# Three chained layers on one core: engine orders planned from a recorded list of operations

## The chip, the cores and the metric

The kernel runs on one core of a Trainium2 chip, in float32 from end to end. The metric is device time in microseconds of that core; three runs before the change gave 747.24 us as their median (746.17 to 747.3).

## The reference

Three layers follow each other, for batch 4, 768 positions and 384 channels: a gated linear recurrence with 8 heads of 48 channels, attention with four experts of which each position uses two, and a two-layer MLP with a residual.

```python
for t in range(S):                                   # recurrence, 8 heads
    state = alpha[:, :, t, :, None] * state + k[t] outer v[t]
    y[:, :, t] = q[t] @ state
logits = x @ w_gate                                  # x: y, heads side by side
w = softmax over the two largest logits
for e in range(4):                                   # causal attention, one head of 64 each
    a = softmax(causal((x @ wq[e]) @ (x @ wk[e]).T / 8))
    out += w_e * (a @ (x @ wv[e]) @ wo[e])
xn = layer_norm(out) * g_ln
return out + relu(xn @ w_ch1) @ w_ch2                # 384 -> 1536 -> 384
```

## The kernel before, in words

**Recurrence.** It is computed in 24 chunks of 128 positions (4 batches by 6). For a chunk, `gla_a` makes the running product of the gates (a scan on VectorE, L199), its inverse by a logarithm and an exponential on ScalarE (L201, L202), and scales keys and queries (L203 to L206, partly on GpSimd). `gla_b` multiplies keys by queries (L221) with 48 rows of the array in use, two heads side by side in its upper and lower half, masks the product (L225) and transposes the keys (L230). `gla_c` updates the state (L244, L254, L255) and computes the chunk's output (L263) with 32 columns of the array in use, four products side by side. `qkv` projects two chunks at a time to queries, keys and values (L304, L318).

**Attention.** The 48 units are pairs of experts in one block of 128 query positions (`UN`). `scores` (L432) has 64 rows of the array in use, two experts side by side; the maximum is taken on VectorE (L438, L440) and the exponential on ScalarE (L442). `transp` transposes the result (L464) and `av` multiplies it with the values (L487), 64 columns in use, again two experts side by side; L490 spreads the weights. `wout` (L505) projects the result and stores it to a buffer in DRAM.

**MLP.** 12 blocks of 256 positions: layer norm and its transposes (L611), first product (L631), second product (L648). Its weights arrive as 64-bit floats and are split into two 32-bit parts by `conv` on VectorE, ScalarE and GpSimd (L536 to L550); the first weight goes through DRAM.

**Products.** Where both operands carry 32 bits in full, as in L221, L244, L263, L487 and L490, a matmul of the program shows as two records in the trace. Projections and MLP instead split each operand in a high and a low part and use three matmuls for a product.

**What sets the order.** The program issues its operations in an order in which recurrence and MLP are generators that are pulled a little at a time between the steps of the attention units (`fill`, `pull`, `need`). That is not yet the order of the engines: the context is made with `schedule_with_timeline_sim=True` (L818), and the library's scheduler sorts every engine's instructions by its own model of times. Only the matmuls of `av` are held together by `manual_schedule` (L482). In this text a **mode** of TensorE is one of four ways in which the array is used: full (128 rows, 128 columns), half (up to 64 rows: L221, L432), pair (64 columns: L487, L490) and quad (32 columns: L263). A **switch** is a place in TensorE's order where a matmul of one mode follows one of another.

```python
            for n, (qt, kt) in enumerate(((QH, KH), (QL, KH), (QH, KL))):
                for h in range(2):
                    pe.matmul(P[h][x], qt[rs[h], p, qs], kt[rs[h], p, pw * x:pw * x + pw], ...)   # L432
...
        with tc.manual_schedule(engines={mybir.EngineType.PE}):                                   # L482
...
    with tile.TileContext(nc, schedule_with_timeline_sim=True) as tc:                             # L818
```

Of the kernel before, what the change touches and what calls it, by code (L numbers as in the profile page):

```python
# [21 lines left out]
PF0 = 0.05  # L22
PF1 = 0.98
NA = 4
NAT = 2
MB = 1.0
MB0 = -10000
TM = 4
KP = 0
NF = 8  # L30
LA = 2
SB = 0
KP2 = 1
GE = 1
PS1 = 1
RRE = 0
OLE = 0
CVU = 33
GQ = 0
GST = 0  # L40
HS = 2
EO = 0
LO = 1
OL = 1
CV0 = 0
GAT = 0
G0 = 1
SW = 1
NWU = 40
AF0 = 0  # L50
RB = 2
CB = 1
NB = 1
W2 = 384
CR = 5
B, H, S, D = 4, 8, 768, 48
DM = H * D
# [6 lines left out]
CW = AW + 2 * 512  # L64

# [4 lines left out]

@with_exitstack
def kernel(ctx: ExitStack, tc: tile.TileContext, akq, vd, wqkv, wo, g_ln, w1, w2, out):
    nc = tc.nc
    pe, dve, act, pool, sp = nc.tensor, nc.vector, nc.scalar, nc.gpsimd, nc.sync

# [4 lines left out]
    psF = ctx.enter_context(tc.tile_pool(name="psF", bufs=NF, space=PSUM))  # L80
    att_ps = ExitStack()
    gen_st = [ExitStack()]
    gen_pool = {}
    gen_pool[1] = ctx.enter_context(tc.tile_pool(name="gen1", bufs=1))
    gen_pool[0] = gen_st[0].enter_context(tc.tile_pool(name="gen0", bufs=1, side="right"))
    fill_st = ExitStack()
# [3 lines left out]
    xs = dram.tile([B, S, DM], F32, name="xs")  # L90
# [3 lines left out]
    psx = {}  # L94

    def psf():
        return psF.tile([128, 512], F32, tag="F", name="F")

    def psm():
        return psx["p"].tile([128, 512], F32, tag="X", name="X") if psx and NF < 5 else psf()  # L100

    ld = [gl.tile([128, CW], F32, name=f"ld{i}") for i in range(4)]
    vb = [gl.tile([128, 4, 2, 2, 32], F32, name=f"vb{i}") for i in range(3)]
    st = [gl.tile([128, 4, 3, 32], F32, name=f"st{i}") for i in range(2)]

    def load_sc(c):
        b, s = divmod(c, NSC)
        sp.dma_start(ld[c % 4], akq[b, s])

    def load_vb(c):  # L110
        b, s = divmod(c, NSC)
        sp.dma_start(vb[c % 3].rearrange("p j x h e -> p (j x h e)"), vd[b, s])

    def new_gen(b):
        p = gen_pool[b % 2]
        if (b % 2, "t") not in GEN:
            GEN[b % 2, "t"] = (*(p.tile([128, 2, S], FR, name=f"{n}{b % 2}") for n in ("QH", "QL", "KH", "KL")),
                               p.tile([128, NSC, E * HD + E], F32, name=f"V{b % 2}"),
                               p.tile([128, NSC, E], F32, name=f"W{b % 2}"))
        GEN[b] = GEN[b % 2, "t"]  # L120
# [5 lines left out]
    GEN = {}  # L126
    wraw = []
    for k in range(KT):
        t = aw.tile([128, 772], F32, name="A", bufs=NA)
        sp.dma_start(t, wqkv[:, k])  # L130
        wraw.append(t)
# [3 lines left out]
    gsb = const.tile([128, KT], F32, name="gsb")  # L135
    sp.dma_start(gsb, g_ln)

    ident = const.tile([128, 128], F32, name="ident")
    make_identity(nc, ident)
    for _ in range(NWU // 4):  # L140
        P = psf()
        for x in range(4):
            pe.transpose(P[:, 128 * x:128 * x + 128], ident, ident)
    hot = gl.tile([128, 4, 129], F32, name="hot")
    pool.memset(hot, 0.0)
    pool.memset(hot[:, :, 0:1], 1.0)
    for t in st:
        pool.memset(t, 0.0)
    gmask = gl.tile([128, 128], F32, name="gmask")
    pool.memset(gmask, -1.0)  # L150
    pool.affine_select(out=gmask, in_=gmask, pattern=[[1, 128]], compare_op=OP.is_ge, fill=0.0, base=0,
                       channel_multiplier=-1)
    cmask = const.tile([128, 512], BF, name="cmask")
    pool.memset(cmask, 0.0)
    pool.affine_select(out=cmask[:, 384:], in_=cmask[:, 384:], pattern=[[-1, 128]], compare_op=OP.is_ge, fill=-1e9, base=0,
                       channel_multiplier=1)
    tri = const.tile([128, 4, 4], F32, name="tri")
    pool.memset(tri, 1.0)
    pool.affine_select(out=tri, in_=tri, pattern=[[1, 4], [-1, 4]], compare_op=OP.is_gt, fill=0.0, base=0,
                       channel_multiplier=0)  # L160

    g20 = const.tile([128, KT], F32, name="g20")
    pool.tensor_scalar(g20, gsb, 2.0 ** -20, 0.0, op0=OP.mult, op1=OP.add)

    WH = gl.tile([128, KT, 772], FR, name="WH")
    WL = gl.tile([128, KT, 772], FR, name="WL")
    OWH = const.tile([128, 2, DM], FR, name="OWH")
    OWL = const.tile([128, 2, DM], FR, name="OWL")

    def split_w():  # L170
        for k in range(KT):
            act.activation(WH[:, k], wraw[k], AF.Copy)
            (dve if SW else pool).tensor_tensor(WL[:, k], wraw[k], f(WH[:, k]), op=OP.subtract)
        if not OL:
            load_wo()

    def load_wo():
        oraw = aw.tile([128, 2 * S], F32, name="at", bufs=NAT)[:, :2 * DM].rearrange("p (k c) -> p k c", k=2)
        sp.dma_start(oraw, wo)
        act.activation(OWH, oraw, AF.Copy)  # L180
        pool.tensor_tensor(OWL, oraw, f(OWH), op=OP.subtract)

    G = {}
    SM = {}
    XT = {}

    def gla_a(c):
        s = c % NSC
        t = ld[c % 4]
        al = t[:, 0:AW]  # L190
        q = t[:, AW:AW + 512].rearrange("p (j t) -> p j t", j=4)
        k = t[:, AW + 512:].rearrange("p (j t) -> p j t", j=4)
        gt = gw.tile([128, 4, 129], F32, name="gt", bufs=3)
        gi = gw.tile([128, 4, 129], F32, name="gi")
        gm = al[:, :512].rearrange("p (j t) -> p j t", j=4)
        G[c] = gt
        for j0, j1 in (((0, 2), (2, 4)) if c < HS else ((0, 4),)):
            js = slice(j0, j1)
            dve.tensor_tensor_scan(gt[:, js].rearrange("p j t -> p (j t)"), al[:, 129 * j0:129 * j1],  # L199
                                   hot[:, js].rearrange("p j t -> p (j t)"), 0.0, op0=OP.mult, op1=OP.add)  # L200
            act.activation(gi[:, js], gt[:, js], AF.Ln)  # L201
            act.activation(gi[:, js], gi[:, js], AF.Exp, scale=-1.0)  # L202
            (dve if c < G0 else pool).tensor_tensor(gm[:, js], gt[:, js, 1:], gi[:, js, 1:], op=OP.mult)  # L203
            (pool if KP else dve).tensor_tensor(k[:, js], k[:, js], gi[:, js, 1:], op=OP.mult)
            dve.scalar_tensor_tensor(k[:, js], gm[:, js], 2.0, k[:, js], op0=OP.subtract, op1=OP.mult)
            (dve if GQ else pool).tensor_tensor(q[:, js], q[:, js], gt[:, js, 1:], op=OP.mult)  # L206

    def qk_of(c):
        t = ld[c % 4]
        q = t[:, AW:AW + 512].rearrange("p (j t) -> p j t", j=4)  # L210
        k = t[:, AW + 512:].rearrange("p (j t) -> p j t", j=4)
        return q, k

    def gla_b(c):
        q, k = qk_of(c)
        SM[c] = gw.tile([128, 2, 4, 128], F32, name="smk")
        P = [psf().rearrange("p (j t) -> p j t", j=4) for h in range(2)]
        for j in range(4):
            for h in range(2):
                r = slice(64 * h, 64 * h + 48)  # L220
                pe.matmul(P[h][:, j], k[r, j], q[r, j], start=True, stop=True)  # L221
            if j == 1:
                yield 850
        for h in range(2):
            dve.tensor_tensor(SM[c][:, h], P[h], gmask[:, None, :].to_broadcast([128, 4, 128]), op=OP.mult)  # L225
        yield 850
        if c % NSC < NSC - 1:
            P = psf()
            for j in range(4):
                pe.transpose(P[:, 128 * j:128 * j + 128], k[:, j, :], ident)  # L230
            kt = gw.tile([128, 4, 128], F32, name="kt")
            act.activation(kt.rearrange("p j t -> p (j t)"), P, AF.Copy, scale=-1.0)
            G[c, "kt"] = kt
            yield 430

    def gla_c(c):
        s = c % NSC
        q, k = qk_of(c)
        v = vb[c % 3]
        if s < NSC - 1:  # L240
            P = psf()
            kt = G.pop((c, "kt"))
            for j in range(4):
                pe.matmul(P[:, 128 * j:128 * j + 128], kt[:, j, :], v[:, j].rearrange("p x h e -> p (x h e)"), start=True, stop=True)  # L244
            P = P.rearrange("p (j b e) -> p j b e", j=4, b=4)
            new = st[(c + 1) % 2]
            for h in range(2):
                r = slice(64 * h, 64 * h + 48)
                bs = slice(h, 3, 2 - h)
                gl_b = G[c][r, :, 128:129, None].to_broadcast([48, 4, 2, 32])  # L250
# [14 lines left out]
        for T in range(2):  # L265
            jobs = []
            for n in range(4):
                j, h = 2 * T + n // 2, n % 2
                l = [(v[:, j, 0, h], sm[:, h, j])]
                if s:  # L270
                    l.append((sto[:112, j, h], q[:112, j]))
# [4 lines left out]
        for j in range(4):  # L276
            l = [(v[:, j, 1, h], sm[:, h, j]) for h in range(2)]
            if s:
                l.append((sto[:112, j, 2], q[:112, j]))
# [481 lines left out]
    for _ in bk:  # L761
        pass
# [59 lines left out]
```

## Time and profile before

| what | value |
|---|---|
| median of three runs | 747.24 us |
| span of the profiled execution (the page gives no other time of it) | 749.8 us |
| TensorE (PE) busy | 713.5 us, 95% |
| VectorE (DVE) busy | 447.5 us, 60% |
| ScalarE (ACT) busy | 308.5 us, 41% |
| GpSimd (POOL) busy | 174.5 us, 23% |
| matmul records | 6520 |
| mean granted TensorE clock | 0.970 of full |

Matmuls are pipelined: one record reaches from a matmul's start to its modelled end, and the next starts long before that. So the busy share of TensorE says that it is rarely without work and not how fast it works; for that one reads the distance from one start to the next.

### The profile page before, as it was taken

What the parts mean: (1) busy time and instruction counts of PE and PEld (TensorE: products, weight loads), DVE (VectorE), ACT (ScalarE), POOL (GpSimd) and SP (SyncE); (2) the same over time, 40 slices, a digit from 0 to 9 for tenths busy, and PEclk for the clock granted to TensorE, in tenths of its full rate; (3) what the DMA queues carried; (4) which work ended last, traced back from release to release, by engine and by line L of the source; (5) the groups of instructions that cost most, each with busy time, mean ns of one, the idle gap of its engine ahead of it and who ended that gap; (6) DMA issues with size and microseconds to landing.
All of it is one profiled execution on the core that took longest, in us unless ns stands there. A gap on an engine that the chain in (4) does not pass through costs nothing.

```text
span 749.8 us, 16242 instructions
## 1 busy us (share of the span) xinstructions
PE 713.5 (95%) x6520; PEld 643.2 (86%) x6520; DVE 447.5 (60%) x1241; ACT 308.5 (41%) x879; POOL 174.5 (23%) x284
## 2 busy tenths in 40 slices
PE   7599799989989999999899999999999999999998
PEld 6488678868868788779678888999999999999997
DVE  6757787767897787766678954254245335433521
ACT  3324455545555555555567545232223123212310
POOL 4624345243464334321223221000000000000000
PEclk8688999999999999999999999999999999999999
DMA  8113424233322622211932311001100100110100
GB/s 338 71 57 115 151 68 138 98 117 121 121 97 96 208 61 83 77 41 54 323 99 79 96 43 55 22 32 43 43 11 33 43 22 22 43 43 12 32 22 22
DMA packets 30427, 60.87 MB, mean 81 GB/s; under 512 B 2960, under 2 KB 19856, under 8 KB 30352
## 3 DMA queue, kind: packets, MB, share of 16 engines
q1 hardware_dynamic: 18864, 45.68, 18.3%
q10 hardware_dynamic: 8352, 9.44, 3.6%
q0 software_dynamic: 3136, 4.72, 2.3%
q8 instruction: 51, 0.84, 0.5%
q14 instruction: 24, 0.20, 0.1%
HBM read 45.67 MB, written 14.16 MB: 80 GB/s over the span
## 4 chain that ended last, share of the span: by engine, by line
PE 69%; DVE 9%; DMA 7%; ACT 4%; POOL 3%; issue 3%; SPq 0%; ACTq 0%; POOLq 0%; DVEq 0%
PE F L631 21%; PE F L648 20%; PE F L304 5%; PE F L487 5%; PE F L432 4%; PE F L464 3%; DMA ld<-in_akq_dram 3%; PE F L505 2%; DMA raw<-in_w_dram 2%; DVE gt L199 2%; PE F L263 2%; PE F L318 2%; PE F L221 1%; ACT A L442 1%; PE F L244 1%
## 5 line engine op out<-in xcount | busy, mean ns | idle before, releaser
L635 ACT ACTIVATE hh<-F 128x256 fp32r<-128x256 f32 x144 | 55.0, 384 | 196.6 <-PE F L631 196.0
L631 PE MATMUL F<-nh,w1hl 128*128 128x256 f32 x864 | 129.0, 284 | 0.0
L631 PEld LDWEIGHTS F<-nh,w1hl 128*128 128x128 f32 x864 | 114.4, 191 | 1.7 <-issue 0.7
L648 PE MATMUL F<-w2h,hh 128*128 128x384 f32 x288 | 98.8, 343 | 0.0
L648 PE MATMUL F<-w2l,hh 128*128 128x384 f32 x288 | 97.0, 337 | 0.0
L648 PE MATMUL F<-w2h,hl 128*128 128x384 f32 x288 | 96.9, 336 | 0.0
L636 DVE SCALAR_TENSOR_TENSOR hl<-F,hh 128x256 fp32r<-128x256 f32 x144 | 60.1, 419 | 56.8 <-ACT hh L635 56.3
L442 ACT ACTIVATE A<-F,nm 128x384 f32<-128x384 f32 (+4 forms) x128 | 68.4, 541 | 52.7 <-DVE nm L440 44.4
L652 DVE TENSOR_TENSOR xt<-F,xt 128x384 f32<-128x384 f32 x24 | 13.4, 558 | 110.5 <-PE F L648 110.5
L631 PE MATMUL F<-nl,w1hl 128*128 128x256 f32 x432 | 75.5, 283 | 0.0
L487 PE MATMUL F<-at,V 128*64 128x128 f32 x672 | 62.1, 286 | 2.3 <-ACT at L467 1.6
L631 PEld LDWEIGHTS F<-nl,w1hl 128*128 128x128 f32 x432 | 62.2, 192 | 0.2 <-issue 0.2
L487 PEld LDWEIGHTS F<-at,V 128*64 128x64 f32 x672 | 41.5, 137 | 19.1 <-issue 7.5
L464 PE MATMUL F<-ident,A 128*128 128x128 f32 x336 | 54.5, 284 | 3.3 <-DVE rb L494 2.6
L648 PEld LDWEIGHTS F<-w2h,hh 128*128 128x128 f32 x288 | 54.2, 188 | 1.1 <-issue 0.8
L648 PEld LDWEIGHTS F<-w2l,hh 128*128 128x128 f32 x288 | 54.2, 188 | 0.2
L648 PEld LDWEIGHTS F<-w2h,hl 128*128 128x128 f32 x288 | 54.1, 188 | 0.2 <-issue 0.2
L464 PEld LDWEIGHTS F<-ident,A 128*128 128x128 f32 x336 | 37.9, 142 | 12.6 <-issue 5.0
L221 PE MATMUL F<-ld 48*128 48x128 f32 x384 | 37.8, 309 | 9.1 <-issue 5.1
L221 PEld LDWEIGHTS F<-ld 48*128 48x128 f32 x384 | 30.2, 203 | 15.4 <-issue 9.8
L206 POOL TENSOR_TENSOR ld<-ld,gt 128x512 f32<-128x512 f32 (+1 forms) x26 | 30.2, 1166 | 56.4 <-DVE gt L199 29.1
L467 ACT ACTIVATE at<-F 128x512 f32<-128x512 f32 (+1 forms) x72 | 38.7, 542 | 6.6 <-PE F L464 4.8
(185 smaller groups left out, 1420.9 us busy)
## 6 DMA issues: line engine op xcount, KB each, us to landing
ld<-in_akq_dram SPq DMA_DIRECT2D x24, 770.0 KB, 4.8
vb<-in_vd_dram SPq DMA_DIRECT2D x24, 256.0 KB, 2.8
raw<-in_w_dram SPq DMA_DIRECT2D x18, 256.0 KB, 2.7
wsc<-whl ACTq DMA_DIRECT2D x18, 256.0 KB, 2.4
xs<-xo ACTq DMA_DIRECT2D x24, 192.0 KB, 1.9
w1hl<-wsc POOLq DMA_DIRECT2D x4, 1152.0 KB, 14.9
xt<-xs SPq DMA_DIRECT2D x24, 192.0 KB, 2.5
raw<-in_w_dram SPq DMA_DIRECT2D x12, 384.0 KB, 3.2
```

The lines of the kernel that those rows point to most:

```text
L206: (dve if GQ else pool).tensor_tensor(q[:, js], q[:, js], gt[:, js, 1:], op=OP.mult)
L221: pe.matmul(P[h][:, j], k[r, j], q[r, j], start=True, stop=True)
L304: pe.matmul(P[:, mt % 2], wt[:, k, cs], x[:, k], start=(n == 0), stop=(n == 8))
L432: pe.matmul(P[h][x], qt[rs[h], p, qs], kt[rs[h], p, pw * x:pw * x + pw], start=(n == 0), stop=(n == 2), skip_group_check=True)
L442: act.activation(A[h][:, pw * x:pw * x + pw], t, AF.Exp, bias=nm[:, h:h + 1], scale=1.0 if x < npc - 1 else -1.0, accum_out=dn2[:, h, x:x ...
L464: pe.transpose(P[:, 128 * n:128 * n + 128], A[h][:, 128 * x:128 * x + 128], ident)
L467: act.activation(at[:, cs], P[:, :128 * len(g)], AF.Copy)
L487: pe.matmul(O[64 * h:64 * h + 64, :], V[:, x, HD * e:HD * e + HD], at[:, c:c + 128], start=(x == 0), stop=(x == i), skip_group_check=True)
L631: pe.matmul(P, w[:, k, c], x[:, k], start=(n == 0), stop=(n == 8))
L635: act.activation(hh, P, AF.Relu)
L636: dve.scalar_tensor_tensor(hl, P, 0.0, f(hh), op0=OP.max, op1=OP.subtract)
L648: pe.matmul(P, x[:, o], w[:, ff], start=(ff == 0 and n == 0), stop=(ff == KF - 1 and n == 2))
```

## The change

The kernel is written again around a recorder. Every operation (or a group of matmuls that belong together) becomes an `Op` with an engine, a duration, a function that issues it, and the tiles or parts of tiles that it reads and writes. `Plan.run` then goes through time: for each engine it takes, from the operations whose inputs are ready and whose buffers are free, the one that stands first in the order in which the program recorded them, adds its duration from the table, and issues it. For TensorE it prefers an operation of the present mode as long as one of another mode isn't more than 4,000 ns of TensorE work ahead of it in the recorded order (`STICK`), and waits up to 60 ns for one (`LOOK`); a switch costs in the table 95 ns and 27 to 107 ns by mode. The result is taken as it stands: the whole kernel is under `manual_schedule()`.

```diff
+STICK = 4000.0
+LOOK = 60.0
+LOAD = {"full": 90.0, "half": 107.0, "quad": 27.0, "pair": 53.0}
+CHANGE = 95.0
...
+            if e == "PE":
+                s, o = min(((s, o) for s, o in cand if s <= t0 + (LOOK if o.mode == mode else 0.0)),
+                           key=lambda x: (x[1].pos + (STICK if x[1].mode != mode else 0.0), x[1].n))
+            else:
+                s, o = min(((s, o) for s, o in cand if s <= t0), key=lambda x: (x[1].pos, x[1].n))
...
+            if e == "PE" and o.mode != mode:
+                ns += CHANGE + LOAD[o.mode]
+                mode = o.mode
...
-        raw = p.tile([128, cw, 2], I32, name="raw", bufs=RB)
-        if i == 0:
-            pool.tensor_copy(raw[0:1, 0, 0:1].bitcast(F32), M["nm"][0:1, 0:1])
...
-    with tile.TileContext(nc, schedule_with_timeline_sim=True) as tc:
-        tile_gla_moe_attention_mlp_kernel(tc, *args)
+    with tile.TileContext(nc, schedule_with_timeline_sim=True) as tc:
+        with tc.manual_schedule():
+            tile_gla_moe_attention_mlp_kernel(tc, *args)
```

TensorE, VectorE, ScalarE and SyncE have the same number of instructions as before, with the same DMAs. GpSimd has 19 fewer: the 18 copies that held back the loads of the first MLP weight (L526) and one unused scaling (L163). On TensorE the switches are 155 where they were 358: ahead of the first output projection 23 (45 before), from there to the last projection to values 92 (217), after that 40 (96).

The first place is TensorE at the last projections of the recurrence (L304 and L318, now L491 and L512), between them attention's transposes (L464, now L644) and its products with the values (L487, now L669). Before:

```order
L304 MATMUL F<-xl,WH 128x256 x3
L487 MATMUL F<-at,V_377 64x128
L318 MATMUL F<-WH,xh 128x260 x3
L318 MATMUL F<-WL,xh 128x260 x3
L318 MATMUL F<-WH,xl 128x260
L487 MATMUL F<-at,V_377 64x128 x7
L490 MATMUL F<-ident,rr 64x128 x2
L318 MATMUL F<-WH,xl 128x260 x2
L464 MATMUL F<-ident,A 128x128 x4
```

And now:

```order
L491 MATMUL F<-xh,WH 128x256 x3
L491 MATMUL F<-xh,WL 128x256 x3
L491 MATMUL F<-xl,WH 128x256 x3
L669 MATMUL F<-at,V_108 64x128 x6
L672 MATMUL F<-ident,rr 64x128 x2
L601 MATMUL F<-KH_106,QH_104 128x512 x2
```

One unit's products with the values stood in two pieces, of one and of seven matmuls, among the projections (four switches), and now stand in one piece, behind the projections and ahead of the next scores. Over the whole program the products with the values (L487, L490) and with the keys of the recurrence (L221) stood in pieces of an odd number of matmuls, in which one has no partner beside it, 68 times before; now they do nowhere.

The second place is TensorE in the stretch behind the recurrence, where only attention is left until the MLP starts: scores (L432, now L601), transposes, products with the values and output projections (L505, now L691). Before:

```order
L432 MATMUL F<-KL_376,QH_373 128x384
L464 MATMUL F<-ident,A 128x128 x6
L487 MATMUL F<-at,V_377 64x128
L464 MATMUL F<-ident,A 128x128 x4
L487 MATMUL F<-at,V_377 64x128 x6
L432 MATMUL F<-KH_1409,QH_1407 128x384
```

And now:

```order
L691 MATMUL F<-OWL,oh 128x384 x2
L691 MATMUL F<-OWH,ol 128x384 x2
L644 MATMUL F<-ident,A 128x128 x18
L669 MATMUL F<-at,V_108 64x128 x8
L672 MATMUL F<-ident,rr 64x128 x2
L601 MATMUL F<-KH_106,QH_104 128x384 x2
```

Transposes of two units now stand together, 18 in a row (20 at the longest), where they stood in pieces of four and six.

The third place is VectorE near the start, where the scan (L341, was L199) and the state updates (L421, was L254) of the first chunks stand. Now:

```order
L461 TENSOR_TENSOR xl<-F,xh 128x3x128
L717 TENSOR_SCALAR cva<-raw 128x256
L719 SCALAR_TENSOR_TENSOR cva<-raw,cva 128x256
L352 SCALAR_TENSOR_TENSOR ld_89<-ld_89,gi 128x512
L421 TENSOR_TENSOR st_94<-st_93,F 48x4x2x32
L341 SCALAR_TENSOR_TENSOR gt<-ld_86,hot 128x516
```

The conversion of the first piece of MLP weight (L717, was L536) has moved in among the fourth chunk's work; before, it stood behind the first unit's scores.

## Rows read from the trace of the kernel before

**Rows 1.** The page: span, and busy time, share and instructions of each engine.
```profile
span 749.8 us, 16242 instructions
PE 713.5 (95%) x6520; PEld 643.2 (86%) x6520; DVE 447.5 (60%) x1241; ACT 308.5 (41%) x879; POOL 174.5 (23%) x284
```
**Rows 2.** Busy time by stage; PEclk is the granted clock (1.00 is full).
```profile
core 0: us, PE busy (x) PEld busy (x) DVE busy (x) ACT busy (x) POOL busy (x), PEclk, DMA share, GB/s
20.00:100.00 80.00, 65.58 (x721) 56.05 (x714) 55.48 (x128) 30.02 (x77) 33.51 (x45) 0.82 0.28 97
100.00:200.00 100.00, 95.48 (x1116) 80.00 (x1116) 76.55 (x199) 51.16 (x146) 44.31 (x66) 0.98 0.33 108
200.00:300.00 100.00, 94.83 (x1127) 80.02 (x1125) 79.93 (x210) 54.11 (x152) 42.78 (x65) 0.98 0.34 114
300.00:400.00 100.00, 96.30 (x941) 77.18 (x940) 68.50 (x236) 58.12 (x181) 26.13 (x60) 0.98 0.39 116
400.00:480.00 80.00, 80.00 (x631) 70.80 (x632) 51.78 (x159) 39.27 (x117) 18.31 (x28) 1.00 0.20 60
480.00:746.00 266.00, 266.00 (x1889) 265.85 (x1887) 100.55 (x294) 67.30 (x192) 0.00 (x0) 1.00 0.09 30
```
**Rows 3.** Timeline of TensorE at a projection: start, duration to the last end.
```profile
159.29 0.52 PE L304 MATMUL F<-xh,WH 128*128 128x256 f32 x3
159.74 0.43 PE L487 MATMUL F<-at,V 128*64 128x128 f32 x2
160.10 0.62 PE L304 MATMUL F<-xh,WL 128*128 128x256 f32 x3
160.56 0.52 PE L304 MATMUL F<-xl,WH 128*128 128x256 f32 x3
160.91 0.51 PE L304 MATMUL F<-xh,WH 128*128 128x256 f32 x3
161.26 0.39 PE L304 MATMUL F<-xh,WL 128*128 128x256 f32 x2
161.59 1.20 PE L487 MATMUL F<-at,V 128*64 128x128 f32 x17
```
**Rows 4.** The same view at a unit's scores.
```profile
361.30 0.45 PE L432 MATMUL F<-KH,QH 64*128 64x384 f32 x2
361.58 0.34 PE L432 MATMUL F<-KH,QL 64*128 64x384 f32 x2
361.75 0.34 PE L432 MATMUL F<-KL,QH 64*128 64x384 f32 x2
362.03 0.54 PE L487 MATMUL F<-at,V 128*64 128x128 f32 x5
```
**Rows 5.** Waits of TensorE by releaser: us in total, times, longest.
```profile
PE F L304 <- ACT xh L286: 9.6, 4, 3.5
PE F L221 <- issue: 5.1, 1, 5.1
PE F L464 <- DVE rb L494: 2.6, 2, 2.4
```
**Rows 6.** The chain that ended last, at the first output projection: start, us.
```profile
86.53 2.22 PE F L505 x6
```
**Rows 7.** Groups of VectorE: the conversion's first and last, of five.
```profile
L536 DVE TENSOR_SCALAR cva<-raw 128x256 int32<-128x256 int32 x18 | 5.9, 327 | 14.3 <-DMA raw<-in_w_dram 14.3
L550 DVE TENSOR_TENSOR whl<-cvu,cva 128x256 fp32r<-128x256 f32 x18 | 9.6, 534 | 3.0 <-POOL cva L549 2.9
```
**Rows 8.** Busy time by stretch, of the 40 transposes of L143 alone.
```profile
core 0: us, PE busy (x), PEclk, DMA share, GB/s
3.00:7.00 4.00, 4.00 (x21) 1.00 0.99 392
7.20:9.20 2.00, 2.00 (x20) 1.00 1.03 407
```

More of the change, by code (lines that the diff above doesn't have):

```diff
@@ L67, in f, with t_dve, t_act, t_pool @@
+HOP = {"PE": 53.0, "DVE": 35.0, "ACT": 36.0, "POOL": 76.0, "SP": 60.0, "H": 0.0}
+LOAD = {"full": 90.0, "half": 107.0, "quad": 27.0, "pair": 53.0}
+CHANGE = 95.0
 def f(ap):
     return ap.bitcast(F32)
+def t_dve(n):
+    return 67.0 + n / 0.96
+def t_act(n):
+    return 52.0 + n / 1.2
+def t_pool(n):
+    return 80.0 + 2.2 * n
+def t_fr(n):
+    return max(n / 2.4, 107.0) + 13.3
+class Op:
+    __slots__ = ("eng", "ns", "fn", "mode", "pos", "deps", "left", "users", "tiles", "start", "end", "nbytes", "n", "ready", "name")
@@ new lines, with warm @@
+    op("POOL", 3900, setup, w=[K0] + st, name="setup")
+    for _ in range(10):
+        P = psf()
+        def warm(P=P):
+            for x in range(4):
+                pe.transpose(P()[:, 128 * x:128 * x + 128], ident, ident)
+        op("PE", 440, warm, r=[K0], w=[P], mode="full", pos=-1.0, name="warm")
+    WH, WL = (new("gl", [128, KT, 772], FR, n) for n in ("WH", "WL"))
+    OWH, OWL = (new("c", [128, 2, DM], FR, n) for n in ("OWH", "OWL"))
+    for t in (WH, WL, OWH, OWL):
+        t()
@@ L214, in gla_b @@
     def gla_b(c):
[L215 to L223, printed above, removed]
+        L = ld[c % 4]
+        sk = SM[c] = new("gw", [128, 2, 4, 128], F32, "smk", "smk")
@@ new lines, in gla_b, with mm @@
+        P = [psf() for h in range(2)]
+        def mm(j0):
+            q, k = qk_of(c)
+            for j in (j0, j0 + 1):
+                for h in range(2):
+                    r = slice(64 * h, 64 * h + 48)
+                    pe.matmul(P[h]().rearrange("p (j t) -> p j t", j=4)[:, j], k[r, j], q[r, j], start=True, stop=True)
+        for j0 in (0, 2):
+            op("PE", 444, lambda j0=j0: mm(j0), r=[(L, (x, j)) for x in "kq" for j in (j0, j0 + 1)],
+               w=[(P[h], j0) for h in range(2)], mode="half", name=f"sc{c}")
+            yield 850 if j0 == 0 else 0
@@ new lines, in qkv, with pv @@
+        for t in range(2):
+            P = psf()
+            def pv(t=t, P=P):
+                for n, (wt, x) in enumerate(three):
+                    for k in range(KT):
+                        pe.matmul(P()[:, :260], x()[:, k, 128 * t:128 * t + 128], wt()[:, k, 512:772], start=(n == 0 and k == 0),
+                                  stop=(n == 2 and k == 2))
+            op("PE", 9 * t_fr(260), pv, r=[WH, WL, xh, xl], w=[P], mode="full", name=f"v{m}")
+            op("ACT", t_act(260), lambda t=t, P=P: act.activation(V()[:, 2 * w + t], P()[:, :260], AF.Copy), r=[P], w=[(V, 2 * w + t)],
+               name=f"V{m}")
+            yield 1000
@@ new lines, in mm @@
+        def mm():
+            n = 0
+            for x, w in ((oh, OWH), (oh, OWL), (ol, OWH)):
+                for p in range(2):
+                    pe.matmul(P()[:, :DM], x()[:, p], w()[:, p], start=(n == 0), stop=(n == 5))
+                    n += 1
+        op("PE", 6 * t_fr(384), mm, r=[oh, ol, OWH, OWL], w=[P], mode="full", name=f"wo{u2}")
+        xo = new("aw", [128, DM], F32, "xo", "xo")
+        op("ACT", t_act(384), lambda: act.activation(xo(), P()[:, :DM], AF.Copy), r=[P], w=[xo], name=f"xo{u2}")
```

922 lines of the change are left out of this document (506 added, 416 removed).

## The prediction

> **What bounds the kernel now.** I read the page first [rows 1]: TensorE is busy for 95% of 749.8 us, the next engine, VectorE, for 60%. The table by stage [rows 2] then says where TensorE could be quicker. From 480 us to the end it is busy all the time at full clock, and there the order has not one switch of mode: 266 us on which the change has nothing to take hold of. From 100 to 400 us TensorE is busy for 95 to 96% at a granted clock of 0.98, with VectorE at 69 to 80%. From 20 to 100 us it is busy for 82% at a clock of 0.82: there it waits. But a busy TensorE isn't a fast one, so the next view is the timeline, and in it the distance from start to start [rows 3, 4]. In an undisturbed row of projections, three starts take 0.35 us (160.56 to 160.91 to 161.26), 0.117 us each. Around every switch of mode the distances grow, and no view of waits lists that, since the engine counts as busy. Last, the waits that are listed [rows 5]: 9.6 us for the split of a chunk's output (L286), four times, 5.1 us once before the keys' products, 2.6 us at the transposes. All idle time of TensorE is 14.4 us from 20 to 100 us and 13.4 us from 100 to 400 [rows 2], 28 us together.
>
> **The price of a switch.** Eleven projections stand between two pieces of pair mode, from 160.10 to 161.59: 1.49 us [rows 3]. At 0.117 us they need 1.29. The other 0.20 us lie at the block's two ends. The two records of a lone product at 159.74 show the same from the other side: from 159.29 to 160.10 pass 0.81 us, in which three projections (0.35) and two records of 0.11 (0.22) leave 0.24; the gap into the block that follows from the full one, some 0.09, belongs to the block before, so 0.15 is left for this one. A unit's scores [rows 4] run from 361.30 to 362.03, 0.73 us for three pairs that need 0.17 each (361.58 to 361.75): 0.21 over. A block of one mode has one switch at each end and shares each with its neighbour, so these excesses are the price of one switch: 0.15 to 0.21 us. I take 0.18. The 358 switches of before then cost 64 us.
>
> **The change part by part.**
>
> *Fewer switches.* The order shows 203 fewer, in three parts. Ahead of the first output projection, which starts at 86.53 us [rows 6], there are 22 fewer: 22 x 0.18 = 4.0 us. But in that stretch TensorE waits for chunks [rows 2, 5], and time that it saves there may only lengthen a wait; I count half, 2.0, with 0 and 4.0 as the ends. From there to the recurrence's last projection there are 125 fewer: 22.5 us. Here TensorE is busy for 95%, and the switches lie on the path. Behind it 56 fewer: 10.1 us. Together 34.6 us; with 0.15 and 0.21 us, and the ends of the start, 27 to 42.
>
> *Partners side by side.* In 68 places before, a product with the values or with the keys stood in a piece of an odd number, so one had no partner in the other half of the array. Its two records then take 0.11 us each by themselves at 159.74 [rows 3], where with a partner that time would be shared by both: 0.11 us lost for each, 7.4 us. The ends are 0 (if the lone one runs beside the next piece after all) and 7.4.
>
> *Longer stretches of transposes.* Up to 20 stand in a row now. What shows their effect on the clock is the start, where nothing but 40 transposes run [rows 8]: 21 records lie in the 4.0 us from 3 to 7 us, 20 in the 2.0 us from 7.2 to 9.2. [...]
>
> *The loads of the first MLP weight without their gate.* The 18 copies on GpSimd go; with GpSimd at 23% that is worth nothing. In their place, conversions now stand among the first chunks. One takes 0.33 us for its first step, 0.53 for its last [rows 7], and between that for the other three, so about 2.1 us on VectorE. From 20 to 100 us VectorE has 24 of 80 us free [rows 2], so I count nothing; if two conversions delayed the chain of the chunks in full it would be 4.2 us.
>
> *The order of the other engines.* VectorE, ScalarE and SyncE do the same work. VectorE's 76.6 to 79.9 us in each 100 [rows 2] lie in a shorter time: if the 300 us from 100 to 400 become about 270, its share grows from 75% to 83%, which still leaves it room. So the waits are what no row can price, as every engine's order is new. The ends: at best the 28 us fall by half, 14, and with them some of the low clock before 100 us (80 us at 0.82 lose at most 14 us; a third of it is 5), 19 us in all; at worst the waits nearly double, 25. The nearest rows are the same stages, and nothing says that a table of durations must do better or worse than the scheduler's own; I take no change.
>
> *The sum.* 749.8 - 34.6 - 7.4 = 707.8 us of profiled span. The median of the runs lies 2.6 us below the profiled span (747.24 against 749.8), so the forecast is **705 us**. With the ends of the switches and of the partners it is 691 to 720.
>
> **The rivals.**
>
> *Waits go too.* The chunks' chain starts earlier, and TensorE finds something to do in the two-microsecond waits. For it: the order takes long stretches of one kind of work that are ready anyway. Against it: the first 100 us hang on a chain of scan, logarithm, exponential and two multiplications that no order shortens. Half of the waits gone, and a third of what the low clock costs: 705 - 19 = 686 us.
>
> *A new bound.* With TensorE quicker, VectorE, at 80% from 200 to 300 us, and the chain from scores over maximum, exponential and transposes to the values set the pace from 100 to 400 us, and half of the saving comes back as waits: 705 + 21 = 726 us. For it: the attention-only stretch behind the recurrence has little to fill a gap with. Against it: two units are always under way, and VectorE has a fifth of its time free.
>
> *Slower: one wait in every unit.* The order is fixed by a table; if that table has the chain of a unit (L440, L442, then the transposes) too short, TensorE stands at the transposes with everything else queued behind them, as it did once at L464 for 2.4 us [rows 5]. There are 48 units. The saving of 42 us is gone when each unit waits 0.88 us more than before; at 1.1 us each it is 705 + 53 = 758 us. Against it: the waits of that kind come to 2.6 us in all now.
>
> *The clock falls in the transposes.* If transposes didn't hold the full clock, the 336 of attention, now in rows of up to 20, would take twice their 0.11 us: 336 x 0.11 = 37 us, so 742 us. [...] Against it stands the start [rows 8].
>
> *The order isn't the one planned.* The library could still sort. The built program speaks against that: the switches are 155, and no pair is parted. I give it no share beyond the 2% for no change.
>
> **How the numbers follow.** The forecast with its own range, 691 to 720, gets 0.58; waits that go too 0.14; a new bound 0.16; the clock 0.03; a wait in every unit 0.07; no change 0.02. All but the last two are faster, so faster 0.91, same 0.02, slower 0.07; a measurement of this kernel can tell about 0.2% from no change. The range for 8 in 10 takes in the forecast and most of the two cases beside it: 685 to 732. It leaves out the clock, the wait in every unit, no change, and the outer parts of the two neighbours.
>
> **What would show it.** In the profile of the changed kernel, the timeline of TensorE should have 155 places where the distance between starts grows by 0.15 to 0.21 us, the stage behind the recurrence should be shorter by about 10 us, and the pure MLP part should take its 266 us as before. The idle time of TensorE should stay near 28 us outside the first 20. If the waits at the transposes or at the values come to more than 30 us, the rival of the units is right; if the clock is below 0.97 in stretches of transposes, the rival of the clock; if waits at L491 (was L304) for the chunk's output fall to a few us, waits go too. A span above 735 us or below 687 would say that the sum is wrong in kind.

## The result, and the profile after

| | median of runs | ratio to before | profiled span |
|---|---|---|---|
| before, same chip | 746.70 us | | 749.8 us |
| after | 721.26 us (720.78 to 723.74) | 0.965 [0.961, 0.969] | 719.1 us |
| forecast | 705 us (685 to 732) | | 707.8 us |

The change made the kernel faster, and the time lies inside the range. Of the 42 us that the sum promised, 25 came. Between the two profiled spans it is 30.7 us, but the profiled execution of the kernel before was a long one: in every later run the time is 1.7 us above the span, and here the span lies 3.1 us above the median time.

The page of the changed kernel: busy time by engine, the 40 slices of TensorE, VectorE and the granted clock, and the chain that ended last.

```profile
span 719.1 us, 16181 instructions
PE 673.1 (94%) x6520; PEld 632.4 (88%) x6520; DVE 470.8 (65%) x1241; ACT 309.8 (43%) x879; POOL 171.5 (24%) x265
...
PE   7789979889888999998979999999999999999998
...
DVE  6999999989899875556699963424424523533521
...
PEclk8799999999899999999999999999999999999999
...
PE 59%; DVE 20%; issue 4%; ACT 2%; POOL 1%; DMA 1%; DVEq 0%; POOLq 0%; ACTq 0%
```

Against [rows 1] TensorE's busy time is 40 us less with the same 6520 records. VectorE's is 23 us *more*, with the same instructions, and its row of slices reads 9 or 8 from the second slice to the fourteenth. It holds 20% of the chain that ended last (9% on the page of before).

The same by stage (columns as in rows 2; the last two stretches are the one behind the recurrence and the pure MLP):

```profile
20.00:100.00 80.00, 69.97 (x900) 61.84 (x898) 76.27 (x166) 38.98 (x102) 43.78 (x53) 0.94 0.36 116
100.00:200.00 100.00, 87.39 (x1059) 78.78 (x1058) 92.87 (x219) 50.72 (x142) 44.25 (x63) 0.93 0.44 144
200.00:300.00 100.00, 94.52 (x1251) 86.07 (x1253) 79.47 (x207) 57.53 (x158) 38.83 (x61) 0.98 0.25 84
300.00:360.00 60.00, 57.10 (x618) 51.17 (x613) 36.85 (x130) 41.16 (x126) 12.15 (x34) 1.00 0.43 123
360.00:410.00 50.00, 43.78 (x387) 38.03 (x384) 47.82 (x138) 29.20 (x88) 17.13 (x21) 1.00 0.33 92
446.00:716.00 270.00, 269.50 (x1901) 269.17 (x1899) 103.65 (x295) 65.67 (x192) 0.00 (x0) 1.00 0.09 29
```

The first stretch gained [rows 2]: 900 matmul records where there were 721, the clock at 0.94 instead of 0.82. The second lost: 1059 instead of 1116, TensorE idle for 12.6 us instead of 4.5 and the clock at 0.93 instead of 0.98. VectorE is busy for 95% of the first stretch and for 93% of the second. The stretch from 360 us shows the same: VectorE works 47.8 of 50 us and TensorE stands for 6.2. The pure MLP is busy throughout, as before. From 20 to 410 us TensorE stands for 37 us, where the prediction wanted some 28.

What TensorE waited for, by line (total, times, longest, us):

```profile
PE F L373 <- DVE ld L352: 4.9, 3, 3.3
PE F L491 <- DVE xl L461: 3.3, 1, 3.3
...
PE F L669 <- ACT A L616: 2.6, 2, 1.6
...
PE F L644 <- DVE xl L461: 1.4, 2, 1.0
```

Most of the listed waits of a microsecond and more end on VectorE, and none repeats by unit. The 3.3 us before L491 can be followed. First TensorE's timeline, then VectorE's:

```profile
99.48 0.61 PE L373 MATMUL F<-ld 48*128 48x128 f32 x8
103.42 1.01 PE L491 MATMUL F<-xh,WH 128*128 128x256 f32 x3 [3.33 <-DVE xl L461]
```

```profile
100.31 0.91 DVE L537 TENSOR_SCALAR sd<-sd 128x2 f32<-128x2 f32 x1
...
101.45 0.99 DVE L539 TENSOR_TENSOR W<-ex,sd 128x8 f32<-128x8 f32 x1
102.36 0.41 DVE L733 TENSOR_TENSOR whl<-cvu,cva 128x256 fp32r<-128x256 f32 x1
102.80 0.56 DVE L461 TENSOR_TENSOR xl<-F,xh 128x384 fp32r<-128x384 f32 x1
```

The split that TensorE waits for (L461) runs as soon as VectorE gets to it. Ahead of it in VectorE's order stand the router's small operations, two of which take 0.9 and 1.0 us for a few elements, and a step of a weight conversion.

**The account.** I took each distance between two starts on TensorE apart: the steady distance of that kind of matmul, a price of 0.15 to 0.20 us where the mode switches (so the column of switches is their number times a price, and no measurement), and the rest (waits, low clock, missing partners). By region (to the first output projection; to the last projection to values; to the last output projection; to the end), in us:

```
                              before                          after
region                        time  steady  switches  rest    time  steady  switches  rest
to first output projection    86.5    43.2   45=8.5   34.8    74.1    46.0   23=4.2   23.9
to last values               269.9   208.7  217=38.4  22.8   248.8   198.3   92=16.1  34.4
to last output projection    116.2    89.7   96=17.6   8.9   116.5    96.1   40=7.3   13.1
to the end                   273.3   272.8    0        0.5   275.8   273.9    0        1.8
```

Over the whole kernel the switches fell by 36.8 us, the steady work stayed at 614 us (some of it moved between the regions), and the rest rose by 6.2 us: 10.9 less at the start, 11.6 more in the middle, 4.2 more behind the recurrence, 1.3 at the end. The sum had expected the rest to fall by 7.4 with the partners. They did come together: among the 1056 records of products with values and keys, 79 more start within 40 ns of the one before (520 against 441), at 0.11 us each 8.7 us. So the waits and the low clock grew by 14 to 15 us that the sum had at zero. The account goes by the two profiled spans; by the medians, which differ by 25 us and not by 31, the growth would be some 5 us larger.

The theory at this point: the first MLP weight's loads, no longer gated, put the conversions on VectorE where the chunks need it, and they run longer there than the table of durations says. The rivals: the waits come from holding work back for a mode (`STICK`), or the table is wrong elsewhere.

### The profile page after: what moved, and what is told of

It is laid out like the page before. It is cut to its first block, busy times and chain, and to the rows that moved or that the text cites. A ratio compares the mean times of both kernels' runs of the same rounds, so it can differ in the third digit from the quotient of the medians.

```text
span 719.1 us, 16181 instructions
## 1 busy us (share of the span) xinstructions
PE 673.1 (94%) x6520; PEld 632.4 (88%) x6520; DVE 470.8 (65%) x1241; ACT 309.8 (43%) x879; POOL 171.5 (24%) x265
## 4 chain that ended last, share of the span: by engine, by line
PE 59%; DVE 20%; issue 4%; ACT 2%; POOL 1%; DMA 1%; DVEq 0%; POOLq 0%; ACTq 0%
PE F L846 20%; PE F L827 20%; PE F L669 3%; PE F L491 3%; PE F L644 2%; DVE F L612 2%; PE F L601 2%; PE F L691 2%; PE F L434 2%; DVE cvu L722 2%; PE F L512 2%; DVE cva L719 2%; DVE gt L341 1%; ACT A L616 1%; DVE cvu L721 1%
## 5 line engine op out<-in xcount | busy, mean ns | idle before, releaser
L644 PE MATMUL F<-ident,A 128*128 128x128 f32 x336 | 51.6, 282 | 3.6 <-DVE xl L461 1.4
L669 PE MATMUL F<-at,V 128*64 128x128 f32 x672 | 47.4, 280 | 5.5 <-ACT A L616 2.6
L669 PEld LDWEIGHTS F<-at,V 128*64 128x64 f32 x672 | 36.7, 137 | 12.9 <-ACT A L616 3.4
L644 PEld LDWEIGHTS F<-ident,A 128*128 128x128 f32 x336 | 39.3, 144 | 8.9 <-ACT A L616 2.8
L354 POOL TENSOR_TENSOR ld<-ld,gt 128x512 f32<-128x512 f32 (+1 forms) x26 | 30.0, 1157 | 44.0 <-DVE gt L341 19.9
L680 POOL TENSOR_TENSOR ol<-rb,oh 128x128 fp32r<-128x128 f32 x48 | 25.0, 523 | 63.7 <-ACT oh L679 63.6
L373 PE MATMUL F<-ld 48*128 48x128 f32 x384 | 31.0, 294 | 7.1 <-DVE ld L352 4.9
```

What stands on the lines that cost most here:

```text
L354: op("POOL", 1150 * m / 512 + 200 * (m < 512), lambda js=js, q=q: pool.tensor_tensor(q(), q(), gt()[:, js, 1:], op=OP.mult), r=gts + kq, w ...
L373: pe.matmul(P[h]().rearrange("p (j t) -> p j t", j=4)[:, j], k[r, j], q[r, j], start=True, stop=True)
L644: pe.transpose(P()[:, 128 * n:128 * n + 128], A[h]()[:, 128 * x:128 * x + 128], ident)
L669: pe.matmul(P()[64 * h:64 * h + 64, 128:256], V()[:, x, HD * e:HD * e + HD], at()[:, c:c + 128], start=(x == 0), stop=(x == i), skip_group ...
L680: op("POOL", 420, lambda: pool.tensor_tensor(ol()[:, p], rb(), f(oh()[:, p]), op=OP.subtract), r=[rb, (oh, p)], w=[(ol, p)], name=f"ol{u}")
```

## The experiments

**The gate alone, in the changed kernel.** The loads of the pieces of the first weight, and with them their conversions, wait for the newest unit's maximum, as they did before.

```diff
+            M["gate"] = plan.ops[-1]
...
-            nbytes=128 * cw * 8, name=f"raw{n}")
+            nbytes=128 * cw * 8, deps=[] if i else [M["gate"]], name=f"raw{n}")
```

> The changed kernel, and in its plan each load of a piece of the first MLP weight depends on the last maximum (L612) of the newest unit, as the copy on GpSimd had it before; 154 switches. Theory (early conversions fill VectorE in the first 230 us and run 0.3 to 0.4 us an instruction slower beside GpSimd): VectorE's busy time from 20 to 180 us falls from 94% to below 85%, the 18 conversions' four first steps return to some 0.3 to 0.5 us each, TensorE's waits fall by 8 to 16 us, and the time is 705 to 713 us. Rival (the waits come from the fixed order and its table of durations, whatever stands in VectorE): 718 to 724 us.

707.46 us (707.03 to 708.49), ratio 0.946 [0.944, 0.948]: about 14 us less than the change. By stage:

```profile
20.00:100.00 80.00, 69.43 (x912) 62.34 (x900) 74.33 (x166) 37.54 (x101) 46.66 (x54) 0.96 0.36 122
100.00:200.00 100.00, 94.92 (x1226) 85.71 (x1228) 87.97 (x218) 57.80 (x161) 46.67 (x65) 0.98 0.39 129
```

From 100 to 200 us TensorE works 94.9 us instead of 87.4, with 1226 records instead of 1059, and its clock is back at 0.98. In the account above the middle's rest falls from 34.4 to 21.3 us, while the start and the end stay within 3 us. VectorE is still busy for 88 to 93%, where I had expected it to fall below 85%: it isn't the share alone that costs. What changed is what fills it. From 100 to 200 us start 50 steps of conversions, 30.5 us of work; with the gate they are 30, of 16.8 us. The conversions got shorter too. VectorE's groups of the four steps on the first weight, before, after and with the gate (busy us, mean ns | idle before):

```profile
L540 DVE SCALAR_TENSOR_TENSOR cvu<-raw,cvu 128x256 f32<-128x256 uint32 x18 | 8.8, 489 | 1.0
L537 DVE SCALAR_TENSOR_TENSOR cva<-raw,cva 128x256 int32<-128x256 int32 x18 | 7.7, 425 | 0.4
...
L538 DVE TENSOR_SCALAR cvu<-cva 128x256 int32<-128x256 int32 x18 | 5.3, 295 | 0.3
```

```profile
L722 DVE SCALAR_TENSOR_TENSOR cvu<-raw,cvu 128x256 f32<-128x256 uint32 x18 | 14.3, 794 | 0.4
L719 DVE SCALAR_TENSOR_TENSOR cva<-raw,cva 128x256 int32<-128x256 int32 x18 | 10.8, 599 | 0.5
...
L721 DVE TENSOR_SCALAR cvu<-cva 128x256 int32<-128x256 int32 x18 | 8.8, 491 | 0.4
L717 DVE TENSOR_SCALAR cva<-raw 128x256 int32<-128x256 int32 x18 | 7.7, 429 | 0.3
```

```profile
L720 DVE SCALAR_TENSOR_TENSOR cva<-raw,cva 128x256 int32<-128x256 int32 x18 | 10.3, 573 | 0.6
...
L723 DVE SCALAR_TENSOR_TENSOR cvu<-raw,cvu 128x256 f32<-128x256 uint32 x18 | 8.7, 481 | 0.6
L722 DVE TENSOR_SCALAR cvu<-cva 128x256 int32<-128x256 int32 x18 | 7.5, 418 | 0.5
...
L718 DVE TENSOR_SCALAR cva<-raw 128x256 int32<-128x256 int32 x18 | 6.2, 344 | 0.1
```

The four steps came to 27.7 us before (with L536 of [rows 7]), 41.6 after, 32.7 with the gate. The planner's table has them at 334, 334, 205 and 205 ns, 19.4 us. What stretches them shows in the timeline of the changed kernel, VectorE and GpSimd. A step by itself:

```profile
160.02 0.43 DVE L719 SCALAR_TENSOR_TENSOR cva<-raw,cva 128x256 int32<-128x256 int32 x1
...
166.37 1.20 POOL L354 TENSOR_TENSOR ld<-ld,gt 128x512 f32<-128x512 f32 x1 [2.92 <-PE F L434]
...
166.66 1.20 DVE L719 SCALAR_TENSOR_TENSOR cva<-raw,cva 128x256 int32<-128x256 int32 x1
168.13 1.32 POOL L348 TENSOR_TENSOR ld<-gt,gi 128x512 f32<-128x512 f32 x1
168.35 1.39 DVE L722 SCALAR_TENSOR_TENSOR cvu<-raw,cvu 128x256 f32<-128x256 uint32 x1
```

The same L719 takes 0.43 us at 160.02 and 1.20 us at 166.66, where it starts inside a GpSimd operation and ends 0.29 us after that one. L722 at 168.35 ends 0.29 us after GpSimd's L348 in the same way. In both places VectorE's step looks as if it waited for the end of GpSimd's operation; what would make it wait no trace shows.

**The gate alone, in the old kernel.** The 18 copies are taken out and all else is left.

```diff
-        if i == 0:
-            pool.tensor_copy(raw[0:1, 0, 0:1].bitcast(F32), M["nm"][0:1, 0:1])
```

> The kernel before without the 18 copies on GpSimd that held the loads of the first MLP weight back; the library's scheduler then puts the conversions behind one another in the first third of VectorE's order; 357 switches. Theory (early conversions): VectorE above 90% from 20 to 180 us and a time 4 to 16 us above the kernel before, 751 to 763 us. Rival (the gate does not matter): within 2 us of the kernel before.

748.23 us (744.55 to 750.79), ratio 1.000 [0.997, 1.002]. The theory's 751 to 763 us did not come, and the total shows no loss, as the rival had it. In the account, the start's rest rises by 8 us (34.8 to 42.7) and the middle's falls by 10 (22.8 to 12.8). So the start gets slower there too, and the old order gets that time back in the middle, where fewer conversions stand. (The spans differ by 4.8 us, 745.0 against 749.8, and the medians don't, so up to half of what comes back may not be the gate's.) What a gate is worth depends on the order it sits in; why the changed order gets nothing back isn't settled by this run.

**The table instead of the gate.** The conversions' durations on VectorE are put where the trace has them; there is no gate.

```diff
-        op("DVE", 67 + cw / 1.85, lambda: dve.tensor_scalar(a(), ...
+        op("DVE", 120 + 0.85 * cw, lambda: dve.tensor_scalar(a(), ...
-        op("DVE", t_dve(cw), lambda: dve.scalar_tensor_tensor(a(), ...
+        op("DVE", 200 + 1.3 * cw, lambda: dve.scalar_tensor_tensor(a(), ...
...
```

> The changed kernel, ungated, with the conversion's five VectorE durations in the table raised to about what they measure (256 columns: 338, 533, 390, 412 and 424 ns in place of 205, 334, 205, 334 and 334); 158 switches, conversions somewhat later in VectorE's order but still ahead of the gated ones. Theory (the table has the conversions too short, so the plan puts them in front of the recurrence's chain as if they were nearly free): most of the gate's 14 us, 707 to 714 us. Rival (it is their place in the first 230 us that costs, whatever the table says): 716 to 722 us.

713.48 us (712.14 to 715.07), ratio 0.952 [0.947, 0.957]. That is 8 of the gate's 14 us: more than half of the cost goes when the plan reckons with conversions as long as they are. The remainder goes only with the gate.

**No sticking to a mode.** `STICK` and `LOOK` are 0; the table still plans the order, with 291 switches.

```diff
-STICK = 4000.0
-LOOK = 60.0
+STICK = 0.0
+LOOK = 0.0
```

> The changed kernel with STICK and LOOK at 0, so TensorE takes the work that was recorded first; 291 switches of mode in place of 155. Theory (a switch costs 0.15 to 0.21 us and nothing else changes): 136 more switches cost 20 to 29 us, 741 to 750 us. Rival (staying in a mode holds critical work back by up to 4 us and makes the new waits): the waits fall by 10 to 20 us and give back most of it, 724 to 735 us.

730.81 us (729.96 to 731.49), ratio 0.977 [0.974, 0.980]: 9.5 us more than the change for 136 switches more, which at 0.18 us would be 24. So about 15 us of waits go when sticking ends. This run doesn't settle why: sticking may hold work back, or the added switches may fill time in which TensorE would have waited for VectorE anyway. It does not take the place of the gate: all steps of the first weight's conversions but one start before 200 us here, and from 100 to 200 us VectorE is busy for 94% and TensorE has 1085 matmul records, near the 1059 of the change and far from the 1226 with the gate. The first output projection comes at 71.2 us, earlier than in the change, with more switches ahead of it (34). So most of the gain at the start isn't the switches'.

**The plan without its order.** The program is recorded and issued as planned, but the library sorts every engine again.

```diff
-        with tc.manual_schedule():
-            tile_gla_moe_attention_mlp_kernel(tc, *args)
+        tile_gla_moe_attention_mlp_kernel(tc, *args)
```

> The changed kernel with the manual schedule taken off: the plan's order is only the order in which operations are issued, and the library's scheduler sorts every engine again; 196 switches, conversions early as in the kernel before without its gate. Theory (switches and early conversions explain the time): against the kernel before without its gate 161 switches fewer, so some 29 us less than that one, 724 to 734 us. Rival (the plan's table of durations is what saves, not the number of switches): 740 us or more.

739.27 us (737.69 to 741.41), ratio 0.988 [0.985, 0.991], with 196 switches: slower than the theory's range and just under the rival's. The first output projection is back at 88.0 us and the start's rest at 37.4. There are 162 switches fewer than before, 29 us at 0.18, and 9 us came: in an order that the library sorts, with the conversions ungated, waits took the others. The planned order of the engines is worth about 13 us at the start; which engine's order does it was not taken apart.

**The price of a switch by itself.** In the changed kernel one more product of 128 columns, whose result nobody reads, follows each of the 144 groups of the first MLP product; once with all 128 rows, once with 64, which is half mode.

```diff
+                pe.matmul(P()[:, 384:512], t()[:128, 0, 0, c], nh()[:128, 0, :128], start=True, stop=True, skip_group_check=True)
```

```diff
+                pe.matmul(P()[:, 384:512], t()[:64, 0, 0, c], nh()[:64, 0, :128], start=True, stop=True, skip_group_check=True)
```

> The price of a switch by itself, first half: the changed kernel with one extra matmul of 128 columns, in full mode, behind each of the 144 groups of the MLP's first product, into the unused part of the group's PSUM bank; its result isn't used. 155 switches as before. 144 extra matmuls at some 0.06 us: 8 to 10 us more, 729 to 732 us. This is the control for the next run.

> Second half: the same extra matmul with 64 rows in place of 128, so in half mode; 439 switches, 284 more than in the control, all of them where nothing else is waited for. By the price of 0.15 to 0.21 us that was read from the timeline: 43 to 60 us above the control, with 0.18 us 51. Rival (the gaps around a switch overlap with work that follows, so a switch costs less than half of that): under 20 us above the control.

735.20 us (732.71 to 735.69) and 781.51 us (778.54 to 783.36), with 155 and 439 switches: 46.3 us for 284 switches, 0.163 us each. The control took 14 us more than the change, not 8 to 10, so an added product costs about 0.10 us instead of 0.06. The spans, 731.0 and 781.6, differ by more, but the half-mode kernel was already 4.9 us behind at the last projection to values (325.5 against 320.6), with the same switches up to there; from there to the end the difference is 45.7 us, 0.161 each. TensorE's timeline, all rows and then 64:

```profile
514.80 0.22 PE L829 MATMUL F<-nh,w1hl 128*128 128x128 f32 x1
514.86 0.93 PE L827 MATMUL F<-nh,w1hl 128*128 128x256 f32 x6
515.63 0.52 PE L827 MATMUL F<-nl,w1hl 128*128 128x256 f32 x3
515.98 0.22 PE L829 MATMUL F<-nh,w1hl 128*128 128x128 f32 x1
```

```profile
501.02 0.32 PE L829 MATMUL F<-nh,w1hl 64*128 64x128 f32 x1
501.28 0.98 PE L827 MATMUL F<-nh,w1hl 128*128 128x256 f32 x6
502.09 0.51 PE L827 MATMUL F<-nl,w1hl 128*128 128x256 f32 x3
502.54 0.32 PE L829 MATMUL F<-nh,w1hl 64*128 64x128 f32 x1
```

A group takes 1.18 us (514.80 to 515.98) with one mode and 1.52 us (501.02 to 502.54) with two switches in it, 0.17 each. In both kernels TensorE is busy for 220.0 of the 220 us from 480 to 700. This prices one pair of modes, full and half; the others were not priced by themselves.

**Less sticking, and more.** With the gate `STICK` is 2000; with the gate and the table of the last experiment below it is 8000 (each a change of that one number).

```diff
-STICK = 4000.0
+STICK = 2000.0
```

```diff
-STICK = 4000.0
+STICK = 8000.0
```

> The gated kernel with STICK at 2000; 194 switches in place of 154. If staying in a mode holds critical work back, waits fall by about 4 us for the 7 us that 40 more switches cost: 709 to 713 us. If the waits have nothing to do with the mode rule: 714 to 717 us. Below 706 us would say that 4000 is too much.

> The gated kernel with the measured table and STICK at 8000; 120 switches in place of 156. If switches alone counted, 36 fewer would save 6 us: 699 to 701 us. Theory (longer stretches of a mode hold critical work back, as shorter ones freed it with STICK at 2000 and 0): half of it or more goes into waits, 702 to 707 us.

712.16 us (711.25 to 713.60), ratio 0.951 [0.947, 0.955], for 194 switches: 4.7 us more than with 154, the gate alone, where 40 switches are 7 us. 707.33 us (704.35 to 708.97), ratio 0.946 [0.943, 0.949], for 120 switches: nothing won over 156, though 36 switches are 6 us. Past 4000 the waits take what the switches give.

**Without the second weight's conversions.** With the gate; the first four steps of the 12 conversions of the second weight are left out on VectorE, so what it computes is not the layer.

```diff
+        if i == 0:
             op("DVE", 67 + cw / 1.85, lambda: dve.tensor_scalar(a(), ...
...
```

> The gated kernel with the first four of five VectorE steps left out of the 12 conversions of the second MLP weight (their result is then not the weight), about 1.9 us of VectorE for each, 23 us in all, behind the recurrence. Theory (in the stretch of attention alone VectorE, busy with these conversions, is what TensorE waits for, and it took the 10 us that 56 fewer switches had promised there): the time falls by 5 to 10 us, 697 to 702 us. Rival (the waits there are the chain of a unit from scores to values): within 2 us of the gated kernel, 705 to 709 us.

700.18 us (698.79 to 701.99), 7.3 us less than with the gate. The stretch behind the recurrence, with the gate and then without these steps:

```profile
360.00:410.00 50.00, 46.16 (x392) 41.34 (x391) 45.82 (x127) 25.12 (x77) 16.99 (x22) 1.00 0.30 85
```

```profile
360.00:410.00 50.00, 50.00 (x450) 46.38 (x449) 28.75 (x93) 26.65 (x80) 12.55 (x21) 1.00 0.29 84
```

With VectorE at 58% instead of 92% TensorE has no idle time in this stretch. In the account this region's rest falls from 15.5 to 7.7 us.

**Gate and table, and the last step moved.** The gate together with measured durations for the conversions, the keys' scaling, the state and the router; then in that kernel the last step of the second weight's conversions on GpSimd.

```diff
-            op("DVE", t_dve(m) + 80, lambda js=js, k=k: dve.tensor_tensor(k(), k(), gi()[:, js, 1:], op=OP.mult), ...
+            op("DVE", t_dve(m) + 220, lambda js=js, k=k: dve.tensor_tensor(k(), k(), gi()[:, js, 1:], op=OP.mult), ...
...
```

```diff
-        op("DVE", 130 + 1.15 * cw, lambda: dve.tensor_tensor(wl(), uf(), af(), op=OP.add), ...
+        ae, an, at_ = (dve, "DVE", 130 + 1.15 * cw) if i == 0 else (pool, "POOL", 1250)
+        op(an, at_, lambda: ae.tensor_tensor(wl(), uf(), af(), op=OP.add), ...
```

> The gated kernel with the measured durations for the conversions and also for the recurrence's key multiplications, state updates and the small operations of the router on VectorE; 156 switches. If wrong entries make the remaining waits: 698 to 704 us. If the waits are those that any order would have: 705 to 709 us.

> The gated kernel with the measured table, and the last step of the 12 conversions of the second MLP weight moved from VectorE (0.55 us each, 6.6 us in all) to GpSimd. Theory (VectorE is what TensorE waits for behind the recurrence): 1 to 4 us less than the gated kernel with the measured table, 702 to 705 us. Rival (the two engines hinder each other, so GpSimd's step costs VectorE as much as it saves): 705 to 708 us.

705.69 us (704.98 to 707.74), ratio 0.942 [0.938, 0.947], and 707.01 us (706.17 to 707.95), ratio 0.946 [0.945, 0.948]. With the gate the corrected table brings no more that can be told from the gate alone (707.46), and GpSimd's help brings nothing. Gate and table together has the lowest median of the full versions, 44 us below the kernel before in the same comparison (749.63), but it isn't clear of the gate alone.

## Why the prediction was right, and where it failed

**Fewer switches: right.** 0.18 us taken, 0.16 to 0.17 measured for one pair of modes in a row of work that is otherwise the same. For the 203 that is 33 to 35 us, where the sum had 34.6. The view that found it was the distance from start to start, as the busy share shows nothing of it: [rows 1] has 95%, and the half-mode run 100% in its MLP, with switches inside.

**Partners side by side: right in kind.** 79 more records start side by side, 8.7 us where the sum had 7.4. No run isolates it.

**The loads without their gate: the step that failed.** It said "VectorE has 24 of 80 us free [rows 2], so I count nothing", with 4.2 us at worst, for two conversions. In the changed order it cost about 14 us. Three things were missed. The free 24 us were those of the old order: the planned one starts the chunks earlier and fills 76 of the 80 us, and 74 even with the gate. The cost fell not from 20 to 100 us but in the stretch behind it, where TensorE had 4.5 us of slack and VectorE got 30.5 us of conversions. And the steps were priced alone, by [rows 7], though they would now lie beside GpSimd's scaling of the gates: 27.7 us became 41.6. Among them is L719, 0.43 us by itself at 160.02 and 1.20 us beside GpSimd's L354 at 166.66. The durations show that a step can take longer there; why it does no run shows.

With the gate alone the median is 707.46 us against the forecast of 705, 41.4 us below the kernel before in the same comparison (748.83), where the sum had 42. Without this one term the forecast would have been met, though in part by luck, because the next two errors cancel.

**The start: mis-sized.** 2.0 us were counted, half of 22 switches. The first output projection comes 12.4 us earlier, and the account puts 10.9 of that into the rest, not into switches. The run with no sticking keeps this gain (71.2 us), the run that the library sorts loses it (88.0 us): it is the planned order, which the sum had at no change. That was the argument for "waits go too", and it held for this stretch only. (Its sign, fewer waits at L491 for the chunk's output, came half: the listed waits there fell from 9.6 us to 5.5, while new ones came elsewhere.)

**Behind the recurrence: right price, no gain in the region.** 10 us were promised, and the region takes 116.5 us as it took 116.2. The switches did go (10.3 us), but 6.4 us more of steady work now lies in it and 4.2 us more of waits. The run without the second weight's conversions shows, in the gated kernel, what sets these waits: VectorE, whose conversions lie in the attention-only stretch.

**The rivals.** "A new bound", which named VectorE and this stretch, is nearest in mechanism (726 us forecast, 721 measured), but it put the bound down to a shorter time for the same work; here the work itself became longer and came sooner. "One wait in every unit" fell: the waits at L644 and L669 come to 9 us over all 48 units. The clock in transposes fell as well: in the changed kernel 222 of the 266 transposes of L644 that follow another start 0.11 us after it, as those of the second stretch of [rows 8] do, and the clock is 1.00 from 360 to 410 us, where transposes belong to every unit. The sum had no term for it, and none was needed. From 100 to 200 us, where the clock is 0.93, TensorE stands for 12.6 us; with the gate, in an order with as few switches, it stands for 5.1 us there and the clock is 0.98. In the changed kernel it reads 0.57 from 103 to 107, 0.58 from 147 to 151 and 0.51 from 185 to 192 us, each time at the end of waits or between them, of 3.3, of 1.2 and of 1.3 and 1.1 us; nine transposes of L644 in these three places start 0.21 us apart. Not every such wait is followed by a low clock: behind two of 1.4 and 1.6 us it reads 1.00 (220 to 226 us).

**Two slips in the working.** The sum's own range should start at 698 us: 749.8 less 42 for the switches, 7.4 for the partners and 2.6. The 691 takes some 7 us off a second time. And VectorE's 76.6 to 79.9 us hold for two of the three stretches of 100 us; the third has 68.5 [rows 2]. The 75% that follows is right, and neither slip changes the forecast.

**Still open.** Whether sticking makes waits of its own, as no run takes it apart from the switches; why the ungated old kernel recovers in the middle what it loses at the start; and which engine's planned order gives the 13 us at the start.

## What to carry to other kernels

Before counting an operation at nothing because an engine has idle time, ask whether that idle time is still there in the new order, and what the operation will run beside: its duration and the cover both belong to the old schedule. A planner with its own table is only as good as the durations of the operations that collide; correct those from a trace before tuning its rules. A switch of TensorE's mode was invisible in busy time here (100% busy with one every 0.76 us), so count switches in the order and read their price from start-to-start distances.

## What the runs showed of the hardware

How much longer a VectorE step takes beside a GpSimd operation was not expected. Steps of the first weight's conversion that run beside an idle GpSimd and beside a busy one, by how much of the record GpSimd covers in the changed kernel (mean ns, with their number; each step occurs 18 times, and those between 20% and 80% are left out):

```
step   GpSimd under 20%   GpSimd over 80%
L717   284 (13)           1036 (3)
L719   424 (9)             763 (6)
L721   288 (5)             623 (10)
L722   417 (1)             852 (10)
```

Of the 29 steps in the right column 11 took 1.18 to 1.46 us and 18 took 0.29 to 0.75 us, so not every GpSimd operation lengthens the step beside it.

A step made longer also delays what stands behind it in VectorE's order: the split L461, for which TensorE waited 3.3 us, starts at 102.80, behind two router operations of 0.91 and 0.99 us, which lie beside GpSimd operations (L354 from 100.01 us, L348 from 101.14 us) and which took 0.19 and 0.17 us at 84.44 and 85.19 us of the old kernel. And handing a step to GpSimd to relieve VectorE gained nothing here: 707.01 us against 705.69.
